# A down product by Strassen's seven products, and second-stage units split over two steps

**Chip, cores, metric.** One Trainium2 chip (trn2), one core. The time is the device time of the program in microseconds; smaller is better. Most figures are medians of four executions or more.

## The reference

A Fourier filter along the sequence, then a two-layer block, all in fp32:

```python
x: (8, 3008, 256)   filt: (1505, 256) complex   w_in: (256, 2048)   w_out: (2048, 256)
y = irfft(rfft(x, axis=1) * (filt_r + 1j * filt_i), n=3008, axis=1)
h = y.reshape(24064, 256) @ w_in
g = h * clip(h + 3, 0, 6) / 6
out = g @ w_out
```

## The kernel before

The filter is done as a 47 x 64 transform in stages: first-stage units (`a_unit`), second-stage units (`b_unit` forward, the filter on VectorE, `bi_unit` back), then a normalising unit (`n_unit`) that makes 512 tokens of `x` ready. The two-layer block runs over 47 blocks of 512 tokens, each in 8 **steps** (256 columns of the hidden layer at a time): 376 steps. In step i TensorE runs the up product of its own part and the down product of the part of step i-1. The filter's units for the next batches are strewn between the steps by a `plan` of slots, two slots a step. In the timelines below each engine runs its instructions in the order in which the program issues them. A **row** is one of the two instructions that the profile shows for each fp32 matmul; PSUM is the memory, divided into banks, that the matmuls here write to. The up product already uses seven products in place of eight.

```python
    def b_unit(b, i):                      # second stage: 4 rows of TensorE work, 5 operations on VectorE
        ...
        for u in range(2):
            nc.tensor.matmul(ps[:, u, :], tab[:, r + u, :], t2[:, r + u, :], start=True, stop=True)
        nc.vector.tensor_tensor(out=s1, in0=ps, in1=f, op=ALU.mult)                      # L301
        nc.vector.tensor_tensor(out=s2[0:HALF], in0=ps[0:HALF], in1=f[HALF:P], op=ALU.mult)
        nc.vector.tensor_tensor(out=s2[HALF:P], in0=ps[HALF:P], in1=f[0:HALF], op=ALU.mult)
        nc.vector.tensor_tensor(out=y[0:HALF], in0=s1[0:HALF], in1=s1[HALF:P], op=ALU.subtract)
        nc.vector.tensor_tensor(out=y[HALF:P], in0=s2[0:HALF], in1=s2[HALF:P], op=ALU.add)
    ...
    def up_2(k, p):                        # sums of the up product: h0 (L395), later h1 in up_3 (L401)
        ...
    def hswish(k, p, i):                   # ScalarE Relu, then one VectorE operation (L414)
        ...
    def down(k, jt, part):                 # 128 hidden columns: g stationary, 256 columns of w_out moving
        for q in order[2 * part:2 * part + 2]:
            nc.tensor.matmul(po[q // 2][:, q % 2, :], g[:, ts(q, P)], w_out[:, jt, :], ...)     # L425
    ...
        for i in range(len(items) + 1):    # the steps
            up_1; down(.., 0); up_2; down(.., 1); up_3; down(.., 0); up_4; hswish(k, p, 1); down(.., 1)
            for slot in (2 * i, 2 * i + 1):
                for fn, a in plan.get(slot, ()):
                    fn(*a)                 # units of the filter, at the end of the step
```

## Time and profile before

| | before |
|---|---|
| median, us | 2974.95 |
| TensorE busy | 96% |
| VectorE busy | 52% |
| start of the first step, us | 157.7 |
| an ordinary step (no unit at its end), us | 6.48 |

The median is of the runs; the busy shares are from the page, the profiler's summary of one execution. A step runs from the start of its first `al` matmul to that of the next step's; after the first blocks nearly all steps agree with one of about a dozen values to 0.01 us. How the page and the timelines are read is in the prediction below. From about 250 us on TensorE has almost no gaps: nothing on another engine decides the time there.

### The profile page before, as it was taken

What the parts mean: (1) busy time and instruction counts of PE and PEld (TensorE: products, weight loads), DVE (VectorE), ACT (ScalarE), POOL (GpSimd) and SP (SyncE); (2) the same over time, 40 slices, a digit from 0 to 9 for tenths busy, and PEclk for the clock granted to TensorE, in tenths of its full rate; (3) what the DMA queues carried; (4) which work ended last, traced back from release to release, by engine and by line L of the source; (5) the groups of instructions that cost most, each with busy time, mean ns of one, the idle gap of its engine ahead of it and who ended that gap; (6) DMA issues with size and microseconds to landing.
All of it is one profiled execution on the core that took longest, in us unless ns stands there. A gap on an engine that the chain in (4) does not pass through costs nothing.

```text
span 2972.5 us, 35295 instructions
## 1 busy us (share of the span) xinstructions
PE 2856.9 (96%) x13440; PEld 2433.2 (82%) x13440; DVE 1537.3 (52%) x2535; ACT 1315.3 (44%) x2622; POOL 321.6 (11%) x580
## 2 busy tenths in 40 slices
PE   3569999999999999999999999999999999999998
PEld 1348888888888888888888888888888888888887
DVE  4774763356533665346643466435663356634343
ACT  1124444444444444444444444444444444444444
POOL 2242001200012000110002100030000200000000
PEclk9679999999999999999999999999999999999999
DMA  7543321313113231232212322133211322110000
GB/s 209 171 114 104 108 81 45 108 61 109 41 46 100 72 104 34 76 77 91 84 29 83 79 91 74 29 97 85 91 57 47 98 73 90 38 29 22 22 8 15
DMA packets 102955, 222.07 MB, mean 75 GB/s; under 512 B 19264, under 2 KB 54786, under 8 KB 102786
## 3 DMA queue, kind: packets, MB, share of 16 engines
q1 hardware_dynamic: 68226, 129.08, 15.2%
q0 software_dynamic: 27904, 80.25, 9.7%
q10 hardware_dynamic: 6656, 10.49, 1.1%
q8 instruction: 106, 1.74, 0.2%
q14 instruction: 63, 0.52, 0.1%
HBM read 140.58 MB, written 79.17 MB: 74 GB/s over the span
## 4 chain that ended last, share of the span: by engine, by line
PE 92%; DVE 4%; DMA 2%; issue 1%; ACT 0%; ACTq 0%; SPq 0%; POOL 0%; POOLq 0%; DVEq 0%
PE po L425 43%; PE al L373 22%; PE be L373 16%; PE psf L313 4%; PE psf L294 4%; PE psn L358 3%; PE psf L268 2%; DMA z_tmp<-t 1%; DVE s L303 0%; DVE s L302 0%; DVE s L301 0%; DMA xc<-in_x_dram 0%; DVE y L304 0%; DVE rest L219 0%; DVE h L395 0%
## 5 line engine op out<-in xcount | busy, mean ns | idle before, releaser
L425 PE MATMUL po<-w_out,g 128*128 128x256 f32 x6016 | 1546.8, 380 | 0.0
L425 PEld LDWEIGHTS po<-w_out,g 128*128 128x128 f32 x6016 | 1145.4, 190 | 156.4
L414 DVE SCALAR_TENSOR_TENSOR g<-r,h 128x512 f32<-128x512 f32 x752 | 520.0, 692 | 531.2 <-ACT r L413 531.2
L413 ACT ACTIVATE r<-h,half_c 128x512 f32<-128x512 f32 x752 | 542.8, 722 | 416.8 <-DVE h L395 404.4
L373 PE MATMUL al<-xt,w_in 128*128 128x256 f32 x2256 | 674.2, 381 | 24.5 <-DVE h L401 24.5
L395 DVE TENSOR_TENSOR h<-be,s 128x512 f32<-128x512 f32 x376 | 260.0, 691 | 584.6 <-PE be L373 581.2
L373 PEld LDWEIGHTS al<-xt,w_in 128*128 128x128 f32 x2256 | 427.2, 190 | 88.2 <-DVE h L401 28.9
L373 PE MATMUL be<-xn,w_in 128*128 128x256 f32 x1504 | 447.7, 379 | 0.1
L373 PEld LDWEIGHTS be<-xn,w_in 128*128 128x128 f32 x1504 | 285.9, 190 | 39.6 <-issue 0.5
L407 ACT ACTIVATE h<-al 128x256 f32<-128x256 f32 x376 | 144.1, 383 | 344.5 <-PE al L373 344.5
L394 ACT ACTIVATE s<-al 128x256 f32<-128x256 f32 x376 | 144.1, 383 | 342.0 <-PE al L373 341.9
L401 DVE TENSOR_TENSOR h<-al,s 128x256 f32<-128x256 f32 x376 | 159.4, 424 | 141.7 <-PE al L373 137.5
L373 PE MATMUL al<-xn,w_in 128*128 128x256 f32 x752 | 229.9, 387 | 0.0
L373 PE MATMUL be<-xt,w_in 128*128 128x256 f32 x752 | 224.2, 380 | 0.0
L385 ACT ACTIVATE s<-be 128x256 f32<-128x256 f32 x376 | 144.1, 383 | 160.6 <-PE be L373 155.8
L438 POOL DMA_DIRECT2D out_dram<-o x112 | 59.6, 537 | 1288.2 <-ACT s L385 432.2
L282 POOL DMA_DIRECT2D z_tmp<-t x336 | 164.8, 498 | 269.8 <-ACT t L271 256.9
L384 ACT ACTIVATE s<-al 128x256 f32<-128x256 f32 x376 | 144.0, 383 | 106.1 <-PE al L373 106.1
L373 PEld LDWEIGHTS al<-xn,w_in 128*128 128x128 f32 x752 | 136.4, 191 | 50.0 <-ACT r L413 15.4
L294 PE MATMUL psf<-t,wb 96*128 96x256 f32 x512 | 145.7, 410 | 30.6 <-DMA t<-z_tmp 18.2
L313 PE MATMUL psf<-y,wi 128*96 128x256 f32 x512 | 143.9, 407 | 22.2 <-DVE s L303 14.5
L373 PEld LDWEIGHTS be<-xt,w_in 128*128 128x128 f32 x752 | 143.2, 190 | 20.2
(42 smaller groups left out, 1422.9 us busy)
## 6 DMA issues: line engine op xcount, KB each, us to landing
ft<-f_tmp SPq DMA_DIRECT2D x56, 512.0 KB, 3.5
xc<-in_x_dram SPq DMA_DIRECT2D x88, 256.0 KB, 3.6
z_tmp<-t POOLq DMA_DIRECT2D x336, 64.0 KB, 2.3
t<-z_tmp SPq DMA_DIRECT2D x56, 384.0 KB
g_tmp<-t POOLq DMA_DIRECT2D x56, 384.0 KB, 4.9
t<-g_tmp SPq DMA_DIRECT2D x160, 128.0 KB, 4.2
out_dram<-o POOLq DMA_DIRECT2D x80, 256.0 KB, 3.7
wb<-wb_t SPq DMA_DIRECT2D x64, 192.0 KB, 5.8
```

The source lines that it names most:

```text
L282: q.dma_start(z_d[b, :, r0 + h * H:r0 + h * H + 2, :], t[p0:p0 + 32, h, :, :])
L294: nc.tensor.matmul(ps[:, u, :], st["tab", b, c][0][:, r + u, :], st["t2", b, c][:, r + u, :], start=True, stop=True)
L313: nc.tensor.matmul(ps[0:KR, u, :], st["tab", b, c][1][:, r + u, :], y[:, u, :], start=True, stop=True)
L373: nc.tensor.matmul(ps, w_in[p][:, w, :], x, start=start, stop=stop, skip_group_check=True)
L385: nc.scalar.activation(out=s5, in_=be[:, 1, :], func=AXT.Copy)
L394: nc.scalar.activation(out=s[:, 1, :], in_=al, func=AXT.Copy)
L395: nc.vector.tensor_tensor(out=h[0].rearrange("p (a n) -> p a n", a=2), in0=be, in1=s, op=ALU.add)
L401: nc.vector.tensor_tensor(out=st["h"][1][:, 256:512], in0=al, in1=s5, op=ALU.add)
L407: nc.scalar.activation(out=st["h"][1][:, 0:256], in_=al, func=AXT.Copy)
L413: nc.scalar.activation(out=r, in_=h, func=AXT.Relu, bias=half_c, scale=1.0 / 6.0)
L414: nc.vector.scalar_tensor_tensor(out=g, in0=r, scalar=1.0, in1=h, op0=ALU.min, op1=ALU.mult)
L425: nc.tensor.matmul(po[q // 2][:, q % 2, :], g[:, ts(q, P)], w_out[:, jt, :], start=(jt == 0 and q % 2 == 0), stop=(jt == JT - 1 and q % 2 ...
```

## The change

The intent is to take an eighth of the down product's multiplications away, as the up product does already: for each 256 hidden columns, 7 products of half the width replace 8 row groups. Seven sums are kept over a whole block in four PSUM banks. For that VectorE must form three sums of g in each step, and six sums for the output at each block's end. To make room there, a second-stage unit is split: its three products in one step, its two y operations at the end of the next, its second matmul after that. The diff, cut to its core:

```diff
-    gp = pool("gp", 3)          psO = pool("psO", 2, space=PSUM)
+    gp = pool("gp", 2)          psO = pool("psO", 1, space=PSUM)      # four tiles: 4 banks, as before
-    w_out = const.tile([P, JT, D], FP32, name="w_out")
+    w_out = [const.tile([P, 7, P], FP32, name="w_out%d" % p) for p in range(NP)]   # sums made by GpSimd
+    def y_unit(b, i):           # the two y operations, cut out of b_unit
...
+    def g_sums(k, p):
+        hswish(k, p, 1)
+        v.tensor_tensor(out=g[:, G1, :], in0=g[:, G3, :], in1=g[:, G22, :], op=ALU.add)
+        v.tensor_tensor(out=g[:, G3:G2 + 1:2, :], in0=g[:, G3:G1 + 1, :],
+                        in1=g[:, G11:G11 + 1, :].broadcast_to([P, 2, 256]), op=ALU.subtract)
+        v.tensor_tensor(out=g[:, G4, :], in0=g[:, G12, :], in1=g[:, G2, :], op=ALU.subtract)
+    def down(k, p, *prods):
+        for n in prods:
+            bank, part = BANK[n]
+            a, w = DOWN[n]
+            for u in range(2):
+                nc.tensor.matmul(st["po", k][bank][:, part, u, :], g[:, a, ts(u, P)], w_out[p][:, w, :], ...)
...
         for n in range(1, B):   # slots of the units
-            gap = 3 (2 for n == 1); first-stage units every 4 slots
+            gap = 4 (3.5 for n == 1); first-stage units every 4 slots, for n == 1 in every slot from 0
             at(s, b_unit, n, i)
-            at(s + gap, bi_unit, n, i)
+            at(s + 2, y_unit, n, i)
+            at(s + 4, bi_unit, n, i)
...
+            up_1; g_sums; down(1); up_2; h0 sum; down(2, 6); up_3 with h1 sum; down(7, 5); up_4; down(4, 3)
+            # out_1 .. out_4: the block's output sums, spread over its last step and the next block's first
```

More of the change, by code (lines that the diff above doesn't have):

```diff
@@ L135 @@
     hp = pool("hp", 2)
-    gp = pool("gp", 3)
+    gp = pool("gp", 2)
     op = pool("op", 2)
@@ L140 @@
     psU = pool("psU", 1, space=PSUM)
-    psO = pool("psO", 2, space=PSUM)
+    psO = pool("psO", 1, space=PSUM)
     wa = const.tile([P, P], FP32, name="wa")
@@ L199, in w_part @@
         src = moe_w_out[ts(p, 2 * P), :].bitcast(I32)
-        return src.rearrange("(a p) d -> p a d", p=P), w_out[:, ts(p, 2), :]
+        return src.rearrange("(a p) d -> p a d", p=P), w_out[p][:, 0:4, :].rearrange("p (a j) m -> p a (j m)", a=2)
     def w_load(i):
@@ L234, in w_conv @@
         nc.gpsimd.tensor_tensor(out=w_part(i)[1], in0=two(rest), in1=two(hi.bitcast(FP32)), op=ALU.mult)
-        if i % 2 == 0:
-            w_sums(w_in[i // 2])
-    def w_sums(w):
-        for o, x0, x1, op_ in ((4, 1, 3, ALU.add), (1, 0, 1, ALU.subtract),
-                               (5, 4, 0, ALU.subtract), (6, 2, 5, ALU.subtract)):
+        w = (w_in, w_out)[i % 2][i // 2]
+        for o, x0, x1, op_ in IN_SUMS if i % 2 == 0 else OUT_SUMS:
             nc.gpsimd.tensor_tensor(out=w[:, o, :], in0=w[:, x0, :], in1=w[:, x1, :], op=op_)
     A11, S3, A12, A22, S1, S2, S4 = range(7)
+    IN_SUMS = ((4, 1, 3, ALU.add), (1, 0, 1, ALU.subtract), (5, 4, 0, ALU.subtract), (6, 2, 5, ALU.subtract))
+    B11, T3, B21, B22, T1, T2, T4 = range(7)
+    OUT_SUMS = tuple((o, x0, x1, ALU.subtract) for o, x0, x1 in ((4, 1, 0), (1, 1, 3), (5, 3, 4), (6, 2, 5)))
+    G11, G3, G1, G2, G4, G12, G22 = range(7)
     def x_load(b, c):
@@ L303, in b_unit @@
         nc.vector.tensor_tensor(out=s2[HALF:P], in0=ps[HALF:P], in1=f[0:HALF], op=ALU.mult)
+        st["y", b, i] = s1, s2, y
+    def y_unit(b, i):
+        s1, s2, y = st["y", b, i]
         nc.vector.tensor_tensor(out=y[0:HALF], in0=s1[0:HALF], in1=s1[HALF:P], op=ALU.subtract)
@@ L394, in up_2, with up_2b @@
         nc.scalar.activation(out=s[:, 1, :], in_=al, func=AXT.Copy)
-        nc.vector.tensor_tensor(out=h[0].rearrange("p (a n) -> p a n", a=2), in0=be, in1=s, op=ALU.add)
         st["h"] = h
+    def up_2b(k, p):
+        al, be, s, s5 = st["up"]
+        nc.vector.tensor_tensor(out=st["h"][0].rearrange("p (a n) -> p a n", a=2), in0=be, in1=s, op=ALU.add)
     def up_3(k, p):
@@ L405, in up_4 @@
         product(al, p, A22, st["xt", k][:, 3, :], stop=True)
+        st["g", k, p] = gp.tile([P, 7, 256], FP32, name="g")
+        relu(0)
         hswish(k, p, 0)
         nc.scalar.activation(out=st["h"][1][:, 0:256], in_=al, func=AXT.Copy)
-    def hswish(k, p, i):
-        h = st["h"][i]
-        r = rp.tile([P, 512], FP32, name="r", tag="r")
-        g = gp.tile([P, 512], FP32, name="g%d" % i)
-        nc.scalar.activation(out=r, in_=h, func=AXT.Relu, bias=half_c, scale=1.0 / 6.0)
-        nc.vector.scalar_tensor_tensor(out=g, in0=r, scalar=1.0, in1=h, op0=ALU.min, op1=ALU.mult)
-        st["g", k, 2 * p + i] = g
@@ L417, in down @@
-    def down(k, jt, part):
-        g = st["g", k, jt]
-        if jt == 0 and part == 0:
-            st["po"] = [psO.tile([P, 2, D], FP32, name="po%d" % i) for i in range(2)]
-        po = st["po"]
-        order = (0, 1, 2, 3) if jt < JT - 1 else (1, 0, 3, 2)
-        for q in order[2 * part:2 * part + 2]:
-            nc.tensor.matmul(po[q // 2][:, q % 2, :], g[:, ts(q, P)], w_out[:, jt, :],
-                             start=(jt == 0 and q % 2 == 0), stop=(jt == JT - 1 and q % 2 == 0))
-        if part == 0:
-            return
-        st.pop(("g", k, jt))
-        if jt < JT - 1:
-            return
-        o = op.tile([P, XC, D], FP32, name="o", tag="o")
-        nc.scalar.activation(out=o[:, 0:2, :], in_=po[0], func=AXT.Copy)
-        nc.vector.tensor_copy(out=o[:, 2:4, :], in_=po[1])
+        relu(1)
@@ new lines, in relu @@
+    def relu(i):
+        r = rp.tile([P, 512], FP32, name="r", tag="r")
+        nc.scalar.activation(out=r, in_=st["h"][i], func=AXT.Relu, bias=half_c, scale=1.0 / 6.0)
+        st["r", i] = r
+    def hswish(k, p, i):
+        o = (G11, G12)[i]
+        nc.vector.scalar_tensor_tensor(out=st["g", k, p][:, o:o + 2, :].rearrange("p a n -> p (a n)"),
+                                       in0=st["r", i], scalar=1.0, in1=st["h"][i], op0=ALU.min, op1=ALU.mult)
+    def g_sums(k, p):
+        hswish(k, p, 1)
+        g = st["g", k, p]
+        v = nc.vector
+        v.tensor_tensor(out=g[:, G1, :], in0=g[:, G3, :], in1=g[:, G22, :], op=ALU.add)
+        v.tensor_tensor(out=g[:, G3:G2 + 1:2, :], in0=g[:, G3:G1 + 1, :],
+                        in1=g[:, G11:G11 + 1, :].broadcast_to([P, 2, 256]), op=ALU.subtract)
+        v.tensor_tensor(out=g[:, G4, :], in0=g[:, G12, :], in1=g[:, G2, :], op=ALU.subtract)
@@ new lines @@
+    BANK = {1: (1, 0), 2: (0, 0), 3: (2, 0), 4: (2, 1), 5: (3, 0), 6: (0, 1), 7: (1, 1)}
+    DOWN = {1: (G11, B11), 2: (G12, B21), 3: (G4, B22), 4: (G22, T4), 5: (G1, T1), 6: (G2, T2), 7: (G3, T3)}
+    OPENS = (2, 1, 4, 5)
+    def down(k, p, *prods):
+        g = st["g", k, p]
+        if p == 0 and 1 in prods:
+            st["po", k] = [psO.tile([P, 2, 2, P], FP32, name="po%d" % i) for i in range(4)]
+        for n in prods:
+            bank, part = BANK[n]
+            a, w = DOWN[n]
+            for u in range(2):
+                nc.tensor.matmul(st["po", k][bank][:, part, u, :], g[:, a, ts(u, P)], w_out[p][:, w, :],
+                                 start=(p == 0 and n in OPENS and u == 0), stop=(p == NP - 1),
+                                 skip_group_check=True)
@@ new lines, in out_1, with o_at, out_2 @@
+    def out_1(k):
+        po = st["po", k]
+        o = op.tile([P, 2, 2, D], FP32, name="o", tag="o")
+        p1 = hp.tile([P, 1, 2, P], FP32, name="p1")
+        nc.scalar.activation(out=p1, in_=po[1][:, 0:1, :, :], func=AXT.Copy)
+        st["o", k] = o, p1
+    def o_at(k, t, d):
+        return st["o", k][0][:, t, :, ts(d, P)]
+    def out_2(k):
+        po = st["po", k]
+        o, p1 = st["o", k]
+        nc.vector.tensor_tensor(out=o[:, 0, :, :].rearrange("p u (d m) -> p d u m", d=2), in0=po[0],
+                                in1=p1.broadcast_to([P, 2, 2, P]), op=ALU.add)
+        nc.vector.tensor_tensor(out=o_at(k, 1, 0), in0=po[1][:, 1, :, :], in1=o_at(k, 0, 1), op=ALU.add)
@@ new lines, in out_3, with out_4 @@
+    def out_3(k):
+        p5 = st["po", k][3][:, 0, :, :]
+        nc.vector.tensor_tensor(out=o_at(k, 1, 1), in0=p5, in1=o_at(k, 1, 0), op=ALU.add)
+        nc.vector.tensor_tensor(out=o_at(k, 0, 1), in0=p5, in1=o_at(k, 0, 1), op=ALU.add)
+    def out_4(k):
+        po = st.pop(("po", k))
+        nc.vector.tensor_tensor(out=o_at(k, 1, 0), in0=po[2][:, 1, :, :], in1=o_at(k, 1, 0), op=ALU.add)
+        nc.vector.tensor_tensor(out=o_at(k, 0, 1), in0=po[2][:, 0, :, :], in1=o_at(k, 0, 1), op=ALU.add)
+        o = st.pop(("o", k))[0].rearrange("p t u d -> p (t u) d")
@@ L482 @@
                 b_unit(0, i)
+                y_unit(0, i)
                 if i % 4 == 2:
@@ L504 @@
             if k in first:
-                at(k * JT - 12, t4_load, k)
+                at(k * JT - (12 if k > 8 else 8), t4_load, k)
                 for dh in range(2):
@@ L514 @@
         for n in range(1, B):
-            t, gap = first[n] * JT - 96, 3
+            tb, gap = first[n] * JT - 88, 4
+            ta = tb - 32
             if n == 1:
-                t, gap = 0, 2
-            tb = t + 32 - 6 * (n == 1)
+                tb, gap, ta = 12, 3.5, 0
             for c in range(NB):
-                at(t + 4 * c, a_unit, n, c)
-                at(t + 4 * c + 2, z_store, n, c)
+                at(ta + (4 if n > 1 else 1) * c, a_unit, n, c)
+                at(ta + (4 if n > 1 else 1) * c + 1, z_store, n, c)
@@ L522 @@
                 if c + 3 < NB:
-                    at(t + 4 * c + 2, x_load, n, c + 3)
+                    at(ta + (4 if n > 1 else 1) * c + 1, x_load, n, c + 3)
             for c in range(TB):
-                at(tb - 6 + 2 * (n == 1), table_load, n, c)
-                at(tb - 6 + 2 * (n == 1), t2_load, n, c)
+                at(tb - 4, table_load, n, c)
+                at(tb - 4, t2_load, n, c)
             for i in range(K2 // 2):
-                s = tb + gap * i
+                s = tb + int(gap * i)
@@ L529 @@
                 at(s, b_unit, n, i)
-                at(s + gap, bi_unit, n, i)
+                at(s + 2, y_unit, n, i)
+                at(s + 4, bi_unit, n, i)
                 if i % 2:
-                    at(s + gap + 1, g_store, n, i // 2)
+                    at(s + 5, g_store, n, i // 2)
                     if i // 2 + TB < NT:
-                        at(s + gap + 1, table_load, n, i // 2 + TB)
-                        at(s + gap + 1, t2_load, n, i // 2 + TB)
+                        at(s + 5, table_load, n, i // 2 + TB)
+                        at(s + 5, t2_load, n, i // 2 + TB)
@@ L536 @@
             if n + 1 < B:
                 for c in range(3):
-                    at(t + 60 + 4 * c, x_load, n + 1, c)
+                    at(first[n + 1] * JT - 140 + 4 * c, x_load, n + 1, c)
         items = [(k, p) for k in range(NBLK) for p in range(NP)]
-        nothing = lambda *a: None
         for i in range(len(items) + 1):
-            k, p = items[i] if i < len(items) else (0, 0)
-            ups = (up_1, up_2, up_3, up_4) if i < len(items) else (nothing,) * 4
-            dn = down if i else nothing
+            up = i < len(items)
@@ L548 @@
+            k, p = items[min(i, len(items) - 1)]
+            dn = i > 0
             kd, pd = items[i - 1]
-            ups[0](k, p)
-            dn(kd, 2 * pd, 0)
-            ups[1](k, p)
-            dn(kd, 2 * pd, 1)
-            ups[2](k, p)
-            dn(kd, 2 * pd + 1, 0)
-            ups[3](k, p)
-            if i < len(items):
-                hswish(k, p, 1)
-            dn(kd, 2 * pd + 1, 1)
+            if up:
+                up_1(k, p)
+            if dn:
+                g_sums(kd, pd)
+                down(kd, pd, 1)
@@ new lines @@
+            if up:
+                up_2(k, p)
+            if pd == NP - 1 and dn:
+                out_1(kd)
+            if dn and pd == 0 and kd:
+                out_3(kd - 1)
+            if up:
+                up_2b(k, p)
+            if dn:
+                down(kd, pd, 2, 6)
+            if up:
+                up_3(k, p)
+            if dn:
+                down(kd, pd, 7, 5)
+                if pd == NP - 1:
+                    out_2(kd)
+                elif pd == 0 and kd:
+                    out_4(kd - 1)
@@ L559 @@
+            if up:
+                up_4(k, p)
+            if dn:
+                down(kd, pd, 4, 3)
             for slot in (2 * i, 2 * i + 1):
@@ L561 @@
                     fn(*a)
+        out_3(NBLK - 1)
+        out_4(NBLK - 1)
 _INS = ['x', 'filt_r', 'filt_i', 'moe_w_in', 'moe_w_out']
```

## The prediction

> **What bounds the kernel now.** I read the page's engine totals, then its chain, then the groups, then two narrow timelines.
>
> ```profile
> span 2972.5 us, 35295 instructions
> PE 2856.9 (96%) x13440; PEld 2433.2 (82%) x13440; DVE 1537.3 (52%) x2535; ACT 1315.3 (44%) x2622; POOL 321.6 (11%) x580
> ...
> PE po L425 43%; PE al L373 22%; PE be L373 16%; PE psf L313 4%; PE psf L294 4%; PE psn L358 3%; PE psf L268 2%; DMA z_tmp<-t 1%; DVE s L303 0%; DVE s L302 0%; DVE s L301 0%; DMA xc<-in_x_dram 0%; DVE y L304 0%; DVE rest L219 0%; DVE h L395 0%
> ...
> L425 PE MATMUL po<-w_out,g 128*128 128x256 f32 x6016 | 1546.8, 380 | 0.0
> L414 DVE SCALAR_TENSOR_TENSOR g<-r,h 128x512 f32<-128x512 f32 x752 | 520.0, 692 | 531.2 <-ACT r L413 531.2
> ```
>
> TensorE is the bound: 96% busy, and the down product alone is 43% of the chain. VectorE has half its time free on average, and waits for others. Each source matmul appears as two rows (fp32, two passes), so the 3008 down matmuls are 6016 rows. The 380 ns is latency; what counts is start to start. The TensorE timeline, one ordinary step (eight make a block of 512 tokens; there are 376), and before it a step's end with extra units:
>
> ```profile
> 1004.36 1.05 PE L358 MATMUL psn<-wai,t 128*128 128x128 f32 x8
> 1005.25 1.03 PE L313 MATMUL psf<-y,wi 128*96 128x256 f32 x4
> 1006.12 1.12 PE L294 MATMUL psf<-t,wb 96*128 96x256 f32 x4
> 1007.07 0.60 PE L373 MATMUL al<-xn,w_in 128*128 128x256 f32 x2
> ...
> 1013.55 0.59 PE L373 MATMUL al<-xn,w_in 128*128 128x256 f32 x2
> ```
>
> From 1007.07 to 1013.55 is 6.48 us for 30 rows of 256 columns: 0.216 us each, without a gap. The eight rows of 128 columns (another stationary tile in each pair) take 1005.25 - 1004.36 = 0.89 us: 0.111 us each, a little over half of 0.216. That is what the new down product will pay per row. A second-stage unit costs eight rows in all (L313 and L294), 8 x 0.216 = 1.73 us. The VectorE timeline of the same step:
>
> ```profile
> 1007.27 0.69 DVE L301 TENSOR_TENSOR s<-psf,ft 128x512 f32<-128x512 f32 x1
> 1008.00 0.68 DVE L302 TENSOR_TENSOR s<-psf,ft 64x512 f32<-64x512 f32 x1
> 1008.69 0.69 DVE L303 TENSOR_TENSOR s<-psf,ft 64x512 f32<-64x512 f32 x1
> 1009.42 0.69 DVE L304 TENSOR_TENSOR y<-s 64x512 f32<-64x512 f32 x1
> 1010.14 0.69 DVE L305 TENSOR_TENSOR y<-s 64x512 f32<-64x512 f32 x1
> 1010.86 0.69 DVE L395 TENSOR_TENSOR h<-be,s 128x512 f32<-128x512 f32 x1
> 1011.59 0.42 DVE L401 TENSOR_TENSOR h<-al,s 128x256 f32<-128x256 f32 x1
> ```
>
> The unit's five operations start 0.20 us after the step does and hold VectorE for 3.6 us. Only then come the two sums of the up product, the second ending at 1012.01, 4.94 us into the step; TensorE needs it at 24 x 0.216 = 5.18. So the old schedule has 0.2 us to spare here: 52% busy hides a place that is nearly tight.
>
> **What the Trainium skill says.** "TensorE: Matmul & The Clock Gate", LDWEIGHTS, gives columns / 1.2 GHz, 107 ns for 128 columns, and says under Back-to-back issue gap that load and matmul together set the spacing. The 0.111 us agrees: at 128 columns load and stream are about equally long, so halving the columns still nearly halves the time. "VectorE: DVE Perf Modes", The perf-mode tier table, has fp32 tensor_tensor in the slowest mode; 0.69 us for 512 elements and 0.42 for 256 agree, so the new sums get no discount. Its section Two Vector instructions with no wait between them says an instruction is held when operands start in another partition quadrant than before; the half-partition operations above do start 0.72 us apart, where the page's ordinary 512-element ones (the first L414 and what follows) can start 0.61 apart. "TensorE", What's actually happening: the clock halves after an idle window of about 3.4 us. The page's PEclk row falls to 6 and 7 only in the first 225 us; stalls near 1 us later should not do it.
>
> **The change, part by part.**
>
> TensorE. A step had 16 down rows of 256 columns (3.46 us); now 7 products x 2 halves x 2 passes = 28 rows of 128 columns (28 x 0.1115 = 3.12). An ordinary step is 6.14 us, 0.333 less. Times 376: **125 us saved**, if nothing else waits. (Counting multiplications, an eighth of 3.46 would be 0.43; the load-paced row takes a quarter of that back.)
>
> VectorE. Per step three sums are added: 256, 512 and 256 elements, each dependent on the one before: starts 0.45, 0.73 and 0.34 us apart (0.42 or 0.69 plus 0.03 for a dependent follower; less 0.08 for an independent one). 376 x 1.5 = 570 us more occupancy. Per block the output takes six operations instead of one copy, about 2.6 us against 0.6: 47 x 2 = 94. VectorE goes to about 2200 us of 3000, still no bound by its mean.
>
> Where it meets TensorE. Each step now wants the second half of the activation and its sums on VectorE early: product 2 at 2.60 us (up_1 1.295, product 1 0.445, up_2 0.865), product 6 at 3.05. In an ordinary step the Relu of the last quarter ends 0.45 us in (0.72 + 0.38 after the product), activation at 0.48, sums at 1.20, 1.66; G2 is ready at 2.35. No stall: 6.14.
>
> The step after a second-stage unit is different. The unit's first three operations come first in VectorE's order: 0.20, 0.92, 1.62. Then the activation 2.35, G1 3.07, G3/G2 3.52 to 4.21. Product 6 can have its weights at about 4.27 (0.06 for the signal, as after L401), plus 0.11 for a load that is no longer hidden. After that TensorE still has products 6, 7, 5, 4, 3 and up_3, up_4: 3.09 us. The step ends at 7.47 instead of 6.14: **1.33 us stall**. The y operations moved to the end of that step (about 7.4 with the activation before them) let the following step's activation start 0.6 to 0.7 us in: no stall there. So a unit's two steps take 7.47 + 6.14 + 1.73 = 15.34 us against 2 x 6.48 + 1.73 = 14.69 before: the split does not cover it. There are 7 x 16 = 112 units inside the loop (batch 0 is before it): **149 us** of stalls.
>
> Smaller terms. In the step where a block's output finishes after a unit (about 26 blocks) four more VectorE operations delay the up sum and hold the single-buffered banks: 0.65 x 26 = 17. The normalising unit's four sums outside unit stretches push the activation to 2.1 us: 1.1 x 19 = 21; at the first unit of a batch 5 us in all. In the first steps the weight conversion (two a step) is already VectorE's; three sums, the second-weight sums on GpSimd (four of 0.62 us) and serial products add about 3 us to each of four or five steps: 14; first-stage units now hidden there: -3. First-stage units later, prologue: 5. Sum: 149 + 17 + 21 + 5 + 14 - 3 + 5 = **208**. Removed besides the 125: the old output copies' waits, at most 10. 2975 - 125 - 10 + 208 = **3048**; I say **3045 us**.
>
> **Rivals.** (a) TensorE stays the bound as the author intends. For: VectorE has 48% free, ordinary steps show slack. Against: its order is fixed, and the first three unit operations plus a four-deep chain come before product 6. It would give 2850 to 2870, above 4% faster. (b) VectorE order is the bound in half the steps: the sum above, about 3045. (c) The row at 128 columns is paced by the 190 ns of the load row instead of 111: a down stage of 28 x 0.19 = 5.3 us, 3600 in all. Against: the eight psn rows above run at 111. (d) Output eviction with four banks instead of two pairs stalls each block. The bank order is staggered (bank 1 and 0 first, 3 and 2 in the next step), and without a unit beside it I get only about 0.1 us; if a full microsecond per block, 40 us more.
>
> **Range and chances.** The 125 and the rows' durations are safe; the uncertain size is the stall per unit. At 0.9 us it gives about 3000; at 1.6, 3078. Early steps are uncertain by 15. That gives 2990 to 3090. Against my sum stands that the slots of the change look tuned by someone, so I leave some chance below. The 2% line is 3034.6: faster 0.03, same 0.41, slower 0.56.
>
> **What would show it.** Down rows x10528 with starts 0.111 apart; ordinary steps (in the last blocks, no units) of 6.14 us; VectorE near 2200 us. Steps after a unit of about 7.5, with TensorE idle twice, released by VectorE's activation and G sums, over 100 us in the waits by name; the chain then carries VectorE lines of the s and g operations at 5% or more. The prediction is wrong if unit steps run without such gaps (then near 2870), if rows of 128 columns are slower than 0.115, or if the clock row drops after the first tenth.

## The result

| | before | changed |
|---|---|---|
| median, us | 2974.95 (4 runs) | 3067.32 (4 runs) |
| ratio | | 1.0308 (95%: 1.029 to 1.0326), slower |
| TensorE busy | 96% | 92% |
| VectorE busy | 52% | 71% |
| an ordinary step, us | 6.48 | 6.15 |
| step after a second-stage unit, us | 6.48 | 7.46 |
| step with a unit's two matmul groups at its end, us | 8.20 | 7.88 |

Ratios in this document are the mean time of one kernel's fast runs over the mean of the other's fast runs of the same rounds, so not quite the ratio of the medians quoted beside them. The result is correct to the reference.

From the page of the changed kernel, the totals, the chain and two groups:

```profile
span 3065.9 us, 45954 instructions
PE 2822.8 (92%) x17952; PEld 2478.2 (81%) x17952; DVE 2191.8 (71%) x3898; ACT 1310.3 (43%) x2622; POOL 340.0 (11%) x612
...
PE 74%; DVE 20%; DMA 3%; issue 2%; ACT 1%; POOL 0%; SPq 0%; ACTq 0%; DVEq 0%; POOLq 0%
PE po L458 34%; PE al L384 18%; PE be L384 10%; PE psf L324 3%; PE psf L301 3%; DVE g L433 3%; DVE g L441 3%; PE psn L369 3%; DVE s L310 3%; DVE s L309 3%; DVE s L308 3%; DVE g L440 2%; PE psf L275 2%; DMA z_tmp<-t 1%; DVE xt L377 1%
...
L458 PE MATMUL po<-w_out,g 128*128 128x128 f32 x10528 | 1474.7, 278 | 113.0 <-DVE g L441 61.0
```

TensorE's own work fell, and the chain left it: VectorE's share of the chain went from 4% to 20%. The lines named are the unit's three products (L308 to L310), the activation (L433) and the added sums (L440, L441). The row pace held: of a step without units, in the TensorE timeline, eight rows of 128 columns take 2857.16 - 2856.26 = 0.90 us, 0.112 each.

```profile
2856.26 1.05 PE L458 MATMUL po<-w_out,g 128*128 128x128 f32 x8
2857.16 0.60 PE L384 MATMUL al<-xt,w_in 128*128 128x256 f32 x2
```

A step after a unit, on TensorE and then on VectorE (it starts at 716.96):

```profile
716.96 0.60 PE L384 MATMUL al<-xn,w_in 128*128 128x256 f32 x2
...
719.14 0.59 PE L384 MATMUL be<-xn,w_in 128*128 128x256 f32 x2
720.04 0.71 PE L458 MATMUL po<-w_out,g 128*128 128x128 f32 x4 [0.30 <-DVE g L433]
721.22 0.71 PE L458 MATMUL po<-w_out,g 128*128 128x128 f32 x4 [0.47 <-DVE g L441]
```

```profile
717.16 0.69 DVE L308 TENSOR_TENSOR s<-psf,ft 128x512 f32<-128x512 f32 x1 [2.70 <-PE psf L301]
717.87 0.68 DVE L309 TENSOR_TENSOR s<-psf,ft 64x512 f32<-64x512 f32 x1
718.56 0.69 DVE L310 TENSOR_TENSOR s<-psf,ft 64x512 f32<-64x512 f32 x1
719.29 0.69 DVE L433 SCALAR_TENSOR_TENSOR g<-r,h 128x512 f32<-128x512 f32 x1
720.02 0.42 DVE L440 TENSOR_TENSOR g<-g 128x256 f32<-128x256 f32 x1
720.48 0.69 DVE L441 TENSOR_TENSOR g<-g 128x512 f32<-128x512 f32 x1
```

VectorE had been idle for 2.70 us until the unit's matmul ended, and then its three products stood in front of the activation. TensorE's two waits end 0.05 to 0.06 us after L433 and L441 do. The numbers in brackets undercount the loss: a row is recorded as longer than its spacing (0.27 against 0.112 us at 128 columns), so part of a wait is hidden under its modelled end, and four rows take 0.71 us after a wait where they take 0.61 without one. The step's length, 7.46 against 6.15, is the true cost: 1.31 us.

Where the 93.4 us between the two profiled spans are, from the steps' starts in the two traces:

| stretch | before | changed | difference |
|---|---|---|---|
| up to the first step | 157.7 | 160.8 | +3.1 |
| block 0 (weights still being converted) | 90.5 | 109.4 | +18.9 |
| blocks 1 to 3 (batch 1's second stage) | 191.2 | 201.5 | +10.3 |
| block 4 | 53.6 | 67.7 | +14.1 |
| blocks 5 to 39 (batches 2 to 7) | 2093.7 | 2152.1 | +58.4 |
| blocks 40 to 46 and the end (no units) | 385.8 | 374.3 | -11.5 |

Part of each difference is work that changed its stretch, not time won or lost; e5 sorts that out.

The windows view over blocks 5 to 39 gives the busy time of TensorE there (after span, the first pair is TensorE's); before, then changed:

```profile
493.00:2586.70 2093.70, 2092.74 (x10014) 1796.46 (x10013) 1085.56 (x1781) 978.66 (x1953) 219.35 (x421) 1.00 0.26 74
```

```profile
539.50:2691.60 2152.10, 2063.20 (x13331) 1827.14 (x13330) 1570.77 (x2795) 969.78 (x1942) 197.60 (x374) 1.00 0.25 70
```

One microsecond idle in 2094 before, 89 after, at the full clock in both. And the waits of TensorE in that stretch, by what ended them (total, times, longest), changed kernel:

```profile
PE po L458 <- DVE g L441: 47.7, 101, 0.5
PE po L458 <- DVE g L433: 33.5, 96, 1.1
PE psn L369 <- ACT t L278: 3.5, 5, 0.7
```

96 is 6 batches x 16 units: one wait for the activation for each unit, and as many for the sums and five more.

### The profile page after: what moved, and what is told of

Its sections match the earlier page's. It is cut to its first block, busy times and chain, and to the rows that moved or that the text cites. A ratio compares the mean times of both kernels' runs of the same rounds, so it can differ in the third digit from the quotient of the medians.

```text
span 3065.9 us, 45954 instructions
## 1 busy us (share of the span) xinstructions
PE 2822.8 (92%) x17952; PEld 2478.2 (81%) x17952; DVE 2191.8 (71%) x3898; ACT 1310.3 (43%) x2622; POOL 340.0 (11%) x612
## 4 chain that ended last, share of the span: by engine, by line
PE 74%; DVE 20%; DMA 3%; issue 2%; ACT 1%; POOL 0%; SPq 0%; ACTq 0%; DVEq 0%; POOLq 0%
PE po L458 34%; PE al L384 18%; PE be L384 10%; PE psf L324 3%; PE psf L301 3%; DVE g L433 3%; DVE g L441 3%; PE psn L369 3%; DVE s L310 3%; DVE s L309 3%; DVE s L308 3%; DVE g L440 2%; PE psf L275 2%; DMA z_tmp<-t 1%; DVE xt L377 1%
## 5 line engine op out<-in xcount | busy, mean ns | idle before, releaser
L458 PEld LDWEIGHTS po<-w_out,g 128*128 128x128 f32 x10528 | 1414.4, 192 | 270.9 <-DVE g L433 97.9
L458 PE MATMUL po<-w_out,g 128*128 128x128 f32 x10528 | 1474.7, 278 | 113.0 <-DVE g L441 61.0
L384 PE MATMUL al<-xt,w_in 128*128 128x256 f32 x2256 | 680.4, 384 | 23.0 <-ACT s L395 19.2
L433 DVE SCALAR_TENSOR_TENSOR g<-r,h 128x512 f32<-128x512 f32 x752 | 518.5, 690 | 210.3 <-ACT r L428 192.4
L384 PEld LDWEIGHTS al<-xt,w_in 128*128 128x128 f32 x2256 | 344.3, 193 | 29.1 <-POOL w_out L238 19.6
L441 DVE TENSOR_TENSOR g<-g 128x512 f32<-128x512 f32 x376 | 261.3, 695 | 12.9
L308 DVE TENSOR_TENSOR s<-psf,ft 128x512 f32<-128x512 f32 x128 | 88.5, 691 | 238.4 <-PE psf L301 235.0
L331 POOL DMA_DIRECT2D g_tmp<-t x56 | 39.3, 702 | 1552.5 <-ACT t L327 1525.9
L395 ACT ACTIVATE s<-al 128x256 f32<-128x256 f32 x376 | 144.2, 384 | 123.6 <-PE al L384 123.6
L443 DVE TENSOR_TENSOR g<-g 128x256 f32<-128x256 f32 x376 | 160.9, 428 | 12.8
```

The source lines that it names most:

```text
L384: nc.tensor.matmul(ps, w_in[p][:, w, :], x, start=start, stop=stop, skip_group_check=True)
L433: nc.vector.scalar_tensor_tensor(out=st["g", k, p][:, o:o + 2, :].rearrange("p a n -> p (a n)"), in0=st["r", i], scalar=1.0, in1=st["h"][i ...
L441: v.tensor_tensor(out=g[:, G3:G2 + 1:2, :], in0=g[:, G3:G1 + 1, :], in1=g[:, G11:G11 + 1, :].broadcast_to([P, 2, 256]), op=ALU.subtract)
L443: v.tensor_tensor(out=g[:, G4, :], in0=g[:, G12, :], in1=g[:, G2, :], op=ALU.subtract)
L458: nc.tensor.matmul(st["po", k][bank][:, part, u, :], g[:, a, ts(u, P)], w_out[p][:, w, :], start=(p == 0 and n in OPENS and u == 0), stop= ...
```

## Experiments

The theory: **VectorE's order** costs the time. A unit's products come first after the step's start, so the activation and the sums, which the changed TensorE order needs early, are late. Its rivals: VectorE has too much work altogether; the single-buffered PSUM banks; the pace of narrow rows; the new places of the units in themselves.

### e1: the split undone

```diff
-                at(s + 2, y_unit, n, i)
+                at(s, y_unit, n, i)
```

> The changed kernel with the split undone: a unit's two y operations follow its three products at once. Theory (order on VectorE): the y operations, 1.44 us, move in front of the activation and the sums that the next step's products 2 and 6 wait for, so a step after a unit goes from 7.46 to about 8.9 us, 112 times: some 3220 us in all. Rival (VectorE simply has too much work): its operations and their total are the same, so the time stays within 0.5% of 3067 us. Rival (PSUM banks or rows of 128 columns): also no change.

Measured: 3282.72 us, 215 more than the changed kernel. VectorE's busy time is the same (2190.6 against 2191.8 us), so its amount of work is not what decides. The split is worth having; it just isn't enough. A step after a unit takes 8.99 us (8.9 expected), but in about one of four the clock adds to it (10.57 in the step shown), and the expectation was 60 us short. The timeline and the windows view (the number before the last two is the granted clock) show why:

```profile
2819.16 0.59 PE L384 MATMUL be<-xn,w_in 128*128 128x256 f32 x2
2821.52 0.71 PE L458 MATMUL po<-w_out,g 128*128 128x128 f32 x4 [1.77 <-DVE g L433]
2822.70 1.17 PE L458 MATMUL po<-w_out,g 128*128 128x128 f32 x4 [0.47 <-DVE g L441]
2823.67 1.06 PE L384 MATMUL al<-xt,w_in 128*128 128x256 f32 x2
```

```profile
2816.00:2823.00 7.00, 4.76 (x24) 3.84 (x24) 6.66 (x12) 1.74 (x4) 0.70 (x1) 0.99 0.20 56
2823.00:2826.40 3.40, 3.40 (x15) 3.22 (x15) 1.82 (x4) 0.72 (x1) 0.00 (x0) 0.53 0.00 0
```

Two idle spells of 1.77 and 0.47 us close together, and TensorE's clock is halved for the next 3.4 us: two rows of 256 columns now take 0.85 us (2823.67 to 2824.52), not 0.43. The trace has 34 such stretches after the first 250 us, about one in each block with units; at half clock each loses some 1.7 us of work, together 60. Not every such pair of spells does it: the step at 2835.42 has 1.84 and 0.47 us and stays at full clock. The 34 stretches start at whole multiples of 3.41 us from one another, so where the spells fall may decide; that is not shown. The changed kernel, with waits of 0.30 and 0.47, has none from block 5 on. So the theory's direction is confirmed, and its size once the clock is added, which I had not counted.

### e2: the products one step later

No operation is removed. The three products get a function of their own, issued after the activation of the following step; the forward matmul of a unit goes last in its slot, so that a PSUM buffer is never asked for before the products that free it.

```diff
+    def s_unit(b, i):      # the three products, cut out of b_unit
...
-                at(s + 2, y_unit, n, i)
-                at(s + 4, bi_unit, n, i)
+                at(s + 2, s_unit, n, i)
+                at(s + 4, y_unit, n, i)
+                at(s + 6, bi_unit, n, i)
...
-                for fn, a in plan.get(slot, ()):
+                for fn, a in sorted(plan.get(slot, ()), key=lambda e: ORDER.get(e[0], 2)):    # y, s first, b last
```

> The changed kernel with a unit's three products one step later on VectorE (after that step's activation instead of ahead of it), y two steps and the second matmul three steps after the first. No operation is removed. Theory (order): the 1.33 us stall in the step after a unit goes; each step of a unit stretch is 6.15 plus 0.87 us; only where the first normalising matmul falls between two units does a PSUM buffer come free late, about 1.4 us once a block. About 2940 us. Rival (VectorE's amount of work): no change from 3067 us. Rival (single PSUM banks for the sums): no change either, since the output's place is the same.

Measured: 2923.65 us (correct), 144 less than the changed kernel, 50 less than the kernel before on the same chip (2973.88), and 16 less than expected. The same sort of step on VectorE (it starts at 689.28):

```profile
693.41 0.42 DVE L420 TENSOR_TENSOR h<-al,s 128x256 f32<-128x256 f32 x1 [0.56 <-PE al L389]
693.75 0.68 DVE L438 SCALAR_TENSOR_TENSOR g<-r,h 128x512 f32<-128x512 f32 x1
694.35 0.68 DVE L313 TENSOR_TENSOR s<-psf,ft 128x512 f32<-128x512 f32 x1
695.05 0.68 DVE L314 TENSOR_TENSOR s<-psf,ft 64x512 f32<-64x512 f32 x1
695.75 0.69 DVE L315 TENSOR_TENSOR s<-psf,ft 64x512 f32<-64x512 f32 x1
696.47 0.69 DVE L438 SCALAR_TENSOR_TENSOR g<-r,h 128x512 f32<-128x512 f32 x1
```

The products now stand at the end of the step, where VectorE has nothing that TensorE waits for; the next step's activation still starts 0.18 us after that step does (696.29). Steps are 7.01 us, 6.15 and four rows, in place of 7.46 and 7.88 in turn. Neither the amount of work nor the PSUM banks changed, so neither rival can explain the 144 us. The y operations and the second matmul came a step later too, which e2 does not separate from the products; e3 leaves them where they were.

### e3: two of the three products left out

Wrong result on purpose (`s2` is `s1` for batches 1 to 7, and L309 and L310 go).

```diff
+        if b:
+            s2 = s1
+        else:
             nc.vector.tensor_tensor(out=s2[0:HALF], ...)
             nc.vector.tensor_tensor(out=s2[HALF:P], ...)
```

> Wrong result on purpose: the changed kernel without two of a unit's three products (1.42 us of VectorE) for batches 1 to 7; y takes its operands from the first product. Theory (order): the activation after a unit starts 1.4 us earlier, the stall vanishes, about 1.3 us for each of 112 units plus the output steps: 2900 us or a little less, and steps after a unit of 6.15 to 6.3 us. Rival (PSUM banks or the row pace of 128 columns): the stall stays and the time is within 1% of 3067 us.

Measured: 2915.32 us; steps after a unit 6.15 us. Leaving the two operations out is worth about as much as moving all three (e2): done at the end of the step, they cost next to nothing, so it was their place that cost.

### e5: the new places with the old down product

The kernel before, with all of the changed kernel's slots and the split of the unit, and nothing else.

> The kernel before (old down product) with the new places of all units alone: y one step after the products, units four slots apart. Theory: the new places cost nothing by themselves, since the old up sums had 0.2 us to spare even with five unit operations in front of them: 2970 to 2985 us, the upper end if the step that holds both normalising matmuls and a first-stage unit runs into the two PSUM buffers (six times 1.6 us). Rival (the new places themselves are what costs): about 3030 us or more.

Measured: 3000.98 us, ratio 1.0092 (95%: 1.0075 to 1.0109). By the 2% rule that is the same, but the interval is clear of 1. The theory is wrong on this point: the places do cost by themselves, 26 us in the profiled span, though less than the rival had it. By stretch e5 takes 17.9 us more than before in block 0, 15.1 more in block 4 and 2.7 less in blocks 5 to 39. Not all of that is waiting. Counted in the traces, the new places (e5's and the changed kernel's alike) bring two first-stage units and 8 second-stage rows into block 0, four units and 12 rows into block 4, and take six first-stage units out of blocks 5 to 39 and 20 rows out of blocks 1 to 3. At 1.21 us for such a unit (two steps of 7.59 and 6.58 against 2 x 6.48) and 0.216 a row, my estimate of the waiting that is left is 14 us in block 0, 8 in block 4, 4 in blocks 5 to 39 and 2 in blocks 1 to 3. In block 0 the waits view shows what did not exist before, ScalarE standing on its store buffers:

```profile
ACT t L271 <- DMA z_tmp<-t: 29.3, 3, 14.2
```

In the changed kernel the same line has 24.6 us:

```profile
ACT t L278 <- DMA z_tmp<-t: 24.6, 3, 11.9
```

Batch 1's first-stage units come two to a step there, and there are two store buffers. The stores are issued by GpSimd, in order, behind weight conversions that wait for VectorE. ScalarE, in order too, waits for a buffer, and TensorE for ScalarE (19.2 us in two waits of the changed kernel). From the changed kernel's timelines of GpSimd and ScalarE:

```profile
210.62 1.40 POOL L234 TENSOR_TENSOR w_in<-rest,bits 128x512 f32<-128x512 f32 x1 [5.10 <-DVE rest L232]
...
215.43 3.45 POOL L289 DMA_DIRECT2D z_tmp<-t  x7
...
221.39 1.09 ACT L278 ACTIVATE t<-psf 128x512 f32<-128x512 f32 x2 [11.88 <-DMA z_tmp<-t]
```

So the added sums, to which the prediction gave the loss in block 0, were not most of it.

### e4: batch 1's first-stage units one to a step

```diff
-                tb, gap, ta = 12, 3.5, 0        # first-stage units in every slot
+                tb, gap, ta = 16, 3, 0          # in every second slot
...              # and 1 -> 2 in the three lines that place them
```

> The changed kernel with the first-stage units of batch 1 one to a step instead of two (their second stage every three slots from slot 16 instead of every 3.5 from 12). Theory: the first eight steps lost 18 to 19 us because ScalarE stands on a store buffer whose stores queue on GpSimd behind the weight conversion (24.6 us of such waits, none before); with one unit a step that wait goes: 3067 - 15 = about 3052 us, the first block 92 to 97 us instead of 109. Rival (the prediction's own term: the conversion plus three more sums and the second weights' sums on VectorE and GpSimd): the first block stays within 3 us of 109.

Measured: 3050.90 us, ratio 1.0259; block 0 took 97.5 us in place of 109.4, and the waits for the store buffers are gone. Blocks 1 to 3 give 4 us back; block 4 takes 59.9 in place of 67.7. e4 moves batch 1's second stage as well (`tb` and `gap` in the diff): by the traces 8 rows left block 0 (1.7 us of the 11.9 gained), 8 left block 4, and all 16 (3.5 us) went to blocks 1 to 3. The bunching is confirmed; 7 us over the 90.5 of before remain in block 0.

### e6: e2, and the normalising units moved too

```diff
-                    at((k - 1) * JT + 6 + 2 * dh, n_unit, k, dh)
+                    at((k - 1) * JT + 8, n_unit, k, dh)
+                at((k - 1) * JT + 12, x_sums, k)     # the four sums of x, cut out of n_unit, two steps later
...
-                    at(k * JT - 4 + dh, n_unit, k, dh)
+                    at(k * JT - c, n_unit, k, dh)     # c = 6, or 4 for batch 1; x_sums at k * JT - 2
```

> e2_s_late, and both normalising matmul groups in one step with the sums of x two steps later, ahead of the other units of the slot. Theory (order on VectorE): the remaining waits of the unit stretches and of the normalising steps go; a block of a unit stretch takes 8 x 6.15 + 4 x 1.73 + 2 x 0.89 = 57.9 us against 58.5 in e2 and 63.9 in the changed kernel; about 2895 us, clearly faster than the kernel before. Rival (the three added sums a step cost TensorE time wherever they stand): no better than e2, 2924 us.

Measured: 2899.12 us (correct), ratio 0.9752 (95%: 0.9735 to 0.9768). A block of a unit stretch takes 58.38 us (expected 57.9). The windows view of blocks 5 to 39:

```profile
520.30:2526.90 2006.60, 2004.07 (x13330) 1831.97 (x13329) 1558.53 (x2797) 959.93 (x1942) 198.40 (x378) 1.00 0.27 76
```

With the same operations TensorE idles 2.5 us, not 89; VectorE does about as much in less time (1558.5 us of work against 1570.8). The stretch is 145.5 us shorter than in the changed kernel and 87.1 shorter than before; some 6 us of the 87.1 are first-stage units that went to earlier blocks (see e5). The rest, about 81 us, is what the change is worth there when no order of issue gives it back.

### e7, e8, e9: the early steps

Three attempts at the rest of the early loss on top of e6. e7 has batch 1's places of e4, and first-stage units of later batches in steps without normalising units:

> e6_spread with the first-stage units of batch 1 one to a step (as in e4) and those of later batches in steps without normalising matmuls. Theory: another 15 us at the start, and the 10.66 us steps (two PSUM buffers for three takers) become about 8 us, 5 or 6 times: about 2865 us, 3.7% faster than before. Rival: the early loss comes from the conversion itself, then only some 10 us below e6.

e8 changes one argument: batch 1's first-stage stores are issued by SyncE in place of GpSimd.

```diff
-    at(ta + (4 if n > 1 else 1) * c + 1, z_store, n, c)
+    at(ta + (4 if n > 1 else 1) * c + 1, z_store, n, c, nc.sync if n == 1 else None)
```

> e6_spread with the first-stage stores of batch 1 issued by SyncE instead of GpSimd, nothing else. Theory: in the first block ScalarE waits 24 us for store buffers because the stores stand behind the weight conversion in GpSimd's order; with another issuer that wait goes and the first block falls from 107 to about 92 us: some 2885 us. Rival (the data's way to memory or the conversion is what takes the time): no change from 2899.

e9 has e4's first-stage units, and batch 1's second stage on even slots only:

> e6_spread with batch 1's first-stage units one to a step and its second stage on even slots only (gaps of 2 and 4 slots), so that no two of its products, y sums and matmuls meet at the end of one step in the wrong order. Theory: the gain of 10 us in the first block is kept and the loss of 5 us that e7 had in blocks 1 to 3 is not: about 2885 us. Rival: the unit rate of two in three steps is too much for VectorE beside the added sums, as in e7: about 2900.

Measured: e7 2901.10 us (0.9756), e8 2892.44 (0.9724; 95%: 0.9709 to 0.9738), e9 2899.54 (0.9751), all correct. Against e6 in the profiled spans, e7 and e9 gain 9 us in block 0 and lose 7 and 9 in blocks 1 to 3, where a unit falls into two steps of three (of e9's 9, 2.6 are 12 rows that moved in). For these two the expectation was a miss; e9's even slots did not help, so the rival (units too dense beside the added sums) fits better. e8 gains the 10 us of block 0 (97.0 against 107.3; 92 was expected) and loses nothing: e6 still has 24.2 us of ScalarE's waits for the store buffers, e8's waits view has none, so the place of the stores in GpSimd's order was that wait. It is the fastest kernel of this study, 2.8% faster than before and 5.7% than the change (2892.44 / 3067.32, medians of different rounds).

## Why the prediction was right

Range and direction held: 3067 measured, 3045 stated, 2990 to 3090. The class was a closer call: slower had 0.56, same 0.41. By its steps:

- **TensorE's saving.** Right for an ordinary step: 6.15 us (6.14 stated). A whole block without units gains less than eight times that, 53.59 - 51.97 = 1.62 us, since the normalising sums (0.81) and the output (0.18) take some back.
- **The stall after a unit.** Right, and the main term. Step 7.46 (7.47 stated), product 6 the last to wait, released by L441 as stated; the two named waits are 61.0 and 50.4 us in the whole run ("over 100"). e1, e2 and e3 show that order on VectorE is its cause: moving the same operations takes it away.
- **No stall in the second step.** Right: 7.88 against 6.14 + 1.73 = 7.87.
- **The step in which the output ends.** Right: 8.14 against 7.47 + 0.65 = 8.12. Without a unit that step takes 6.33 in the changed kernel, 0.18 over (about 0.1 stated), and in e6, beside a unit, 7.38, that is 0.37 over its ordinary 7.01. Single buffering of the four banks can cost no more than that a block (rival d).
- **The old output copies' waits.** Wrong: "at most 10" were taken off, and there are none. The page that the prediction shows has 0.0 idle before L425, and a block without units took 53.59 us, which is 8 x 6.48 + 2 x 0.89 us of rows.
- **The normalising unit's sums.** Mis-sized: 0.81 us a time (6.96 against 6.15), 12 times outside the unit stretches, some 10 us where 1.1 x 19 = 21 was put down.
- **The early steps.** Near in sum, by luck: 14 - 3 + 5 = 16 us were stated, and the time up to the end of block 0 grew by 22. The prediction gave 14 us to the conversion with the added sums and -3 to the bunched first-stage units. e5 has no added sums and still loses 17.9 us in block 0 (some 14 of it waiting); e4, with the sums but without the bunching, is 7 us over the kernel before there. The term with the minus was the cost.
- **Block 4.** Not foreseen: +14.1, of which about 7 is work that moved in. e5 has it too, so it belongs to the places. Its first step takes 13.69 us; in e2, e4 and e6 it is 9.0. In that step TensorE idles 1.23 and 0.67 us, and from 481.5 us on, into the next step, the clock is at half for 6.8 us (the number before the last two):

```profile
481.50:488.30 6.80, 6.13 (x17) 3.54 (x12) 3.26 (x7) 2.06 (x4) 3.94 (x8) 0.50 0.57 172
```

- **The clock.** The prediction held that stalls near 1 us should not halve it. From block 5 on that is so; in block 4 the clock was halved with no idle spell above 1.23 us. Its sign, a drop of the page's clock row after the first tenth, did not show, since 6.8 us are too short for a slice of 77.
- **One more step not foreseen.** Before each batch's first block both normalising groups and a first-stage unit fall into one step. It takes 10.66 us where rows alone give 6.15 + 2 x 0.89 + 1.1 = 9.0, six times: some 10 us. In e6, with the pieces apart, it is 8.04 in five of the six (9.80 in the first, where they still meet), so it goes with the places; that the two PSUM buffers are the reason is argued, not shown.
- **VectorE's mean.** About 2200 us stated, 2191.8 measured. It says nothing about the stall: e6 has it at 75% busy, more than the change's 71%, with 2.5 us of idle TensorE in blocks 5 to 39.
- **Slips that decide nothing.** Rival c's row of 0.19 us would give 2975 + 376 x (5.32 - 3.46) = 3674 us, not 3600. 2870 us, the upper end of rival a, is 3.5% faster, not above 4%. The half-partition operations shown start 0.69 to 0.73 us apart, not always 0.72. The 107 ns that it takes from the skill for a weight load agrees with the spacing of rows, 0.111 us; the load itself is recorded as 190 ns, so that load and stream are equally long is not shown.

The 22 us between 3045 and 3067 are what is left of errors of both signs: by my estimate the copies' waits (+10), the 10.66 us steps (+10) and what is new in block 4 (14.1 - 7.4 moved in + 2.6 saved on its steps - 2.4 counted in the other terms, some +7) against the normalising sums (-11). These leave 16; the rest is not broken down. So the range was met by the main term, and the closeness is in part luck. Against rival (a): the saving is real, and e6 collects it; the change gave it back, mostly through one order of issue.

## What to carry to other kernels

When work moves from the bounding engine to one with free time, ask where in the step the free time is, not how much there is: write down, from the trace, when each result is needed and what stands ahead of it in that engine's order. Put operations nobody waits for directly behind the last one that somebody does wait for. And look at the order of DMA issues too: a store behind a waiting computation holds its buffer, and with it an engine two hops away.

## What the Trainium skill lacked or had wrong

- "TensorE: Matmul & The Clock Gate", What's actually happening, puts the halved clock after an idle window of about 3.4 us. Here idle spells of 1.77 and 0.47 us within such a stretch were enough about one time in four (e1, clock 0.53 for the next 3.4 us), and in block 4 of the changed kernel no spell above 1.23 us came before it; 0.30 and 0.47 us never were from block 5 on. What decides is open. Its section A second HAM failure mode speaks of micro-idles without a size.
- The same page, Back-to-back issue gap, has no fp32 figures. Here a row (one of an fp32 matmul's two) starts every 0.216 us at 256 columns and every 0.111 to 0.112 at 128, each with a weight load of its own; so two half-width rows take 3% longer than one whole.
- "VectorE: DVE Perf Modes" gives no time for a broadcast second operand with a stepped output (another page tells how re-read rows run in the packed modes): the sum L441 is of that form and took 0.695 us, like a plain one of 512 elements (L395 before: 0.691).
- No page read here tells of a store's buffer being held up by its issuing engine's order; it cost ScalarE 24.6 us of waits in the changed kernel, and one argument removed the 24.2 that e6 still had (e8).
